# Strassen's method for half of the last output stage of a sparse-attention and FFN kernel, and one cast moved to another engine

## The chip, the cores and the metric

The kernel runs on one core of one Trainium2 chip. The metric is the device time of one execution in microseconds (us). Engines are named as in the profile: PE is the matrix engine TensorE, PEld its weight loads, DVE is VectorE, ACT is ScalarE, POOL is GpSimd, SP is SyncE, which here issues DMA. SBUF and PSUM are the two on-chip memories of the kernel's tiles; its matmuls write to the PSUM tiles, which the profile's lines name `ps_...`. A "bank" here is a PSUM tile, or the half of one, of 512 fp32 columns of 128 partitions.

## The reference, cut to what matters

```python
def _attn_ref(q, k, v):                       # (8, 8, 576, 64): batch, heads, tokens, head size
    ...                                       # causal; half of the heads local, half strided
    return np.matmul(attn, v)

def _moe_ref(x, w1, w2, w3, w_out):           # x: 4608 tokens x 512
    a = x @ w1                                # first FFN stage, 512 -> 1024
    b = x @ w2
    h = a * b @ w3
    return (h @ w_out).astype(np.float32)     # output, 1024 -> 512
```

Both kernels first fuse `w3 @ w_out` into one 1024x512 weight, called `w34`. What is left for a tile of 512 tokens is the first stage (`a`, `b` and their product `abt`) and the output stage `abt @ w34`. There are nine tiles, 0 to 8. The last two are finished after all attention work and form the tail of the execution.

## The kernel before: the parts that matter

The kernel records its operations in a planner, with the other operations that each depends on. The planner puts them into one fixed order per engine, from estimates of their durations. The framework then derives the semaphore waits between engines from the tiles that each instruction reads and writes, as the built programs of after and e3 show further down. This division is what the explanation turns on: **the planner knows the waits that the author entered, the built program has those that the framework derives.**

The first stage of the last two tiles (`tA`, `tB`) is done by Strassen's method for seven of its eight column blocks of 128. This method multiplies two 2x2 arrangements of blocks with seven block products in place of eight, and pays for it with sums and differences of blocks. Each block takes seven products, P1 to P7, which accumulate in three PSUM banks: A is one tile of its own, E and G are the two halves of one tile of two banks.

```python
SF = cfg.get("sf", ())                                  # (1, 2, 3, 4, 5, 6, 7): column blocks by Strassen
# ... sums and differences of x and of w1, w2 are made by DVE and POOL
def bk(x, kA=kA, kB=kB):
    return bank(*kA) if x == "A" else bank(*kB)[:, "EG".index(x)]
# ... in P5, the first time for a slot:
    seen[plan.slot[kB]] = bank(*kB, [P, 2, NT], FP32)   # one PSUM tile, E is [:, 0], G is [:, 1]
# ...
q1 = prod("P1", take=[kA], rank=R, extra=list(zs.values()))               # A = P1
q5 = prod("P5", take=[kB], rank=R + .1, extra=[q1])                       # G = P5
ce_ = vec("e", "ACT", ... copy("ACT", bk("E"), bk("A")), [q1, q5])        # E = P1
q6 = prod("P6", extra=[ce_], rank=R + .5)                                 # A += P6
c5 = vec("p5", "ACT", ... copy("ACT", new("p5"), bk("G")), [q5], ...)     # p5 to SBUF
q2 = prod("P2", extra=[q5 if n_ < 2 else ce_], rank=R + .6)               # E += P2
cu = vec("u2", "ACT", ... copy("ACT", new("u2"), bk("A")), [q6], ...)     # u2 to SBUF
q7 = prod("P7", extra=[cu], rank=R + 1)                                   # A += P7
g = vec("u4", "DVE", ... tensor_add(bk("G"), bk("G"), tmp["u2"]), [cu, c5], ...)
c11 = vec("c11", "ACT", ... copy("ACT", new("c11"), bk("E")), [q2], ...)  # E to SBUF
c22 = vec("c22", "DVE", ... tensor_add(new("c22"), bk("A"), tmp["p5"]), [q7, c5], ...)
q3 = prod("P3", extra=[g], rank=R + 1.1)                                  # G += P3
q4 = prod("P4", extra=[c22], rank=R + 1.2)                                # A += P4
# h1 = G * c11 and h2 = A * c22 go to abt of tA and tB
```

The lists at the ends are what the planner is told. The output stage is ordinary: for each block `ts` of 128 tokens, eight matmuls of 512 columns, a copy to SBUF and a store of 256 KB.

```python
for ts in range(NT // P):
    ...
    def fo(...):
        for ci in range(4 * hf, 4 * hf + 4):
            pin(nc.tensor.matmul(ps, big[("abt", t)][:, ci, bass.ds(ts * P, P)],
                                 w34[:, ci, bass.ds(n0, nw)], start=(ci == 0), stop=(ci == KF - 1)))
```

The softmax here doesn't subtract the row's maximum and nothing guards it: scores larger than these inputs give would overflow.

## Time and profile before

| | kernel before |
|---|---|
| time, three runs | 270.85 us median (270.61 to 271.14) |
| time of a fourth run, the profiled one | 270.36 us |
| span of its profile, granted clock | 268.3 us, 1.0 |
| tile 7's first product starts | 199.97 us |
| the tail (first product after tile 6's output) starts | 224.71 us |
| last matmul ends | 264.43 us |

The page's own lines are shown in the prediction, further down, with how they are read. Two things are worth seeing beside them. The first is a hole, a time in which TensorE starts nothing, in the timeline of TensorE (columns: start, duration, engine, line, operation, output and inputs, shapes, count):

```profile
236.65 0.59 PE L1053 MATMUL ps_Bw<-st,st 128*128 128x512 f16 x2
237.08 0.59 PE L1053 MATMUL ps_Aw<-st,st 128*128 128x512 f16 x2
237.79 0.59 PE L1053 MATMUL ps_Bw<-st,w2h 128*128 128x512 f16 x2
```

Matmuls overlap here (each of the first two lines lasts 0.59 us, and the second starts 0.43 us after the first), so their durations cannot be added; starts can be subtracted. From 236.65 to 237.08 are 0.43 us, two slots of 0.216 without a hole. From 237.08 to 237.79 are 0.71 us, so 0.28 us are lost. The third line carries no idle note, because by its modelled duration the line ahead of it ended just before. Every hole in this document is found in this way: the difference of two starts, less the count times 0.2157 us (512 columns), 0.1092 (256) or 0.056 (128). In the profiles of before and after matmuls that follow without a hole start 215 or 216 ns apart with 512 columns, 108 to 110 with 256 and 55 or 56 with 128; none starts less than 215 ns after one of 512 columns. The second thing is the end of GpSimd's work, in its timeline:

```profile
232.16 2.13 POOL L965 TENSOR_TENSOR st<-w1h,st 128x1024 f16<-128x1024 f16 x1
```

After 234.3 us this engine is idle, and the change uses that time.

### The profile page before, as it was taken

To read this page: it belongs to the slowest core of one execution; us is meant where nothing else is said; L and a number is where in the kernel's file an instruction comes from. 1 tells how busy PE (TensorE), PEld (TensorE's weight loads), DVE (VectorE), ACT (ScalarE), POOL (GpSimd) and SP (SyncE) were. 2 spreads that over 40 slices of the span, in tenths; PEclk is the share of its full clock that TensorE was granted. 3 is DMA by queue.
4 is the path that set the end of the run, shared out by engine and by line. 5 is a ranking of instruction groups with operands and counts; after the bars stand their busy time and mean duration, and the time that the engine had idled before them with its cause. 6 is when DMAs were issued, how large, how long until landed. Compare 5 with 4: busy or idle time off the path is not lost.

```text
span 268.3 us, 6079 instructions
## 1 busy us (share of the span) xinstructions
PE 256.9 (96%) x2251; PEld 140.3 (52%) x2251; DVE 179.0 (67%) x342; ACT 162.2 (60%) x293; POOL 168.9 (63%) x186
## 2 busy tenths in 40 slices
PE   7878799999999999999999999999999999999994
PEld 2457687545655555554554454455445554434443
DVE  6744565885787748866875788569748865678601
ACT  2780467774766785577477557764775576577241
POOL 6676897779979716955796369716989753900000
PEclk9999999999999999999999999999999999999999
DMA  6999899999799988899999998999996004000053
GB/s 247 322 365 288 294 353 353 326 266 290 255 287 211 175 205 243 188 167 283 228 184 180 264 248 182 189 252 235 162 189 198 2 0 156 0 2 0 0 197 121
DMA packets 72766, 54.41 MB, mean 203 GB/s; under 512 B 44256, under 2 KB 62048, under 8 KB 72736
## 3 DMA queue, kind: packets, MB, share of 16 engines
q1 hardware_dynamic: 72736, 54.02, 83.1%
q8 instruction: 18, 0.29, 0.5%
q14 instruction: 12, 0.10, 0.1%
HBM read 38.93 MB, written 9.44 MB: 180 GB/s over the span
## 4 chain that ended last, share of the span: by engine, by line
PE 86%; DMA 7%; POOL 2%; issue 1%; DVE 1%; ACT 1%; SPq 1%; POOLq 0%; DVEq 0%
PE ps_o L1155 23%; PE ps_b L1135 19%; PE ps_a L1119 18%; DMA st<-in_moe_w_dram 5%; PE ps_Aw L1053 4%; PE ps_S L795 4%; PE ps_Bw L1053 3%; PE ps_mm L670 3%; PE ps_X L843 3%; PE ps_X L831 3%; DMA st<-in_k_dram 2%; PE ps_U L924 2%; PE ps_T L748 2%; POOL w3n L314 1%; SPq L317 1%
## 5 line engine op out<-in xcount | busy, mean ns | idle before, releaser
L1155 PE MATMUL ps_o<-w,abt 128*128 128x512 f16 (+2 forms) x304 | 67.9, 368 | 0.0
L1135 PE MATMUL ps_b<-xT,w2h 128*128 128x512 f16 x232 | 59.4, 379 | 0.2 <-DVE kTL L312 0.2
L1119 PE MATMUL ps_a<-xT,w1h 128*128 128x512 f16 x232 | 59.6, 379 | 0.0
L310 ACT COPY asb<-ps_a 128x512 f32<-128x512 f32 x58 | 33.9, 587 | 30.1 <-PE ps_a L1119 29.0
L1141 DVE TENSOR_TENSOR abt<-ps_b,asb 128x512 f16<-128x512 f32 x58 | 39.9, 688 | 7.8 <-PE ps_b L1135 6.4
L314 POOL CAST xs<-st 80x1024 f16<-80x1024 f32 (+1 forms) x36 | 33.3, 940 | 18.3 <-DMA st<-in_k_dram 10.5
L812 ACT ACTIVATE ps_S<-ps_S 128x576 f32<-128x576 f32 (+2 forms) x56 | 32.8, 627 | 16.4 <-PE ps_S L795 16.4
L1155 PEld LDWEIGHTS <-abt 128*128 128x128 f16 x304 | 27.5, 98 | 28.2 <-issue 0.2
L904 DVE TENSOR_TENSOR xT<-ps_X,rcp 64x288 f16<-64x288 f32 x56 | 25.2, 450 | 18.3 <-ACT rcp L888 17.8
L1135 PEld LDWEIGHTS <-w2h 128*128 128x128 f16 x232 | 21.6, 98 | 23.7 <-issue 0.7
L310 ACT COPY osb<-ps_o 128x512 f32<-128x512 f32 (+1 forms) x36 | 20.2, 580 | 18.7 <-PE ps_o L1155 17.7
L314 POOL CAST v16L<-st 32x768 f16<-32x768 f32 (+1 forms) x32 | 26.3, 821 | 7.3 <-DMA st<-in_v_dram 5.7
L1119 PEld LDWEIGHTS <-w1h 128*128 128x128 f16 x232 | 20.2, 99 | 18.5
L819 DVE TENSOR_TENSOR ptm<-ps_S,maskL 128x576 f16<-128x576 f32 x28 | 19.9, 753 | 9.1 <-ACT ps_S L812 9.0
L867 DVE TENSOR_TENSOR xqs<-ps_X,rcq 96x384 f16<-96x384 f32 (+1 forms) x36 | 20.5, 568 | 1.2
L314 POOL CAST v16S<-st 72x1024 f16<-72x1024 f32 (+1 forms) x16 | 16.5, 1035 | 6.8 <-DMA st<-in_v_dram 6.8
L877 ACT ACTIVATE ps_X<-ps_X 64x576 f32<-64x576 f32 x28 | 17.6, 630 | 3.8 <-PE ps_X L831 3.2
L888 ACT ACTIVATE rcp<-ps_X 64x576 f32<-64x576 f32 x28 | 18.1, 647 | 0.9
L843 PEld LDWEIGHTS <-ptm 128*96 128x96 f16 (+1 forms) x224 | 14.6, 123 | 5.8 <-issue 0.2
L670 PE MATMUL ps_mm<-woh,xT 128*128 128x256 f16 x128 | 16.0, 273 | 1.3 <-POOL woh L314 1.3
L314 POOL CAST x<-st 128x1024 f16<-128x1024 f32 x14 | 14.4, 1036 | 4.4 <-DMA st<-in_k_dram 2.6
L819 DVE TENSOR_TENSOR ptm<-ps_S,maskK 72x576 f16<-72x576 f32 x20 | 14.1, 746 | 2.6 <-ACT ps_S L812 2.6
(113 smaller groups left out, 359.1 us busy)
## 6 DMA issues: line engine op xcount, KB each, us to landing
out_dram<-osb SPq DMA_DIRECT2D x35, 256.0 KB
st<-in_moe_w_dram SPq DMA_DIRECT2D x16, 512.0 KB
st<-in_v_dram SPq DMA_DIRECT2D x16, 288.0 KB
st<-in_v_dram SPq DMA_DIRECT2D x16, 256.0 KB
st<-in_q_dram SPq DMA_DIRECT2D x7, 512.0 KB
st<-in_k_dram SPq DMA_DIRECT2D x7, 512.0 KB
st<-in_q_dram SPq DMA_DIRECT2D x10, 256.0 KB
st<-in_k_dram SPq DMA_DIRECT2D x10, 256.0 KB
```

What stands on the lines that cost most here:

```text
L310: pin(nc.scalar.copy(out=out, in_=in_))
L314: pin(nc.gpsimd.tensor_copy(out=out, in_=in_))
L670: pin(nc.tensor.matmul(ps, w3T(kc)[:, js], big["woh"][:, kc, ns], start=(kc == 0), stop=(kc == KF - 1)))
L812: pin(nc.scalar.activation(out=sps, in_=sps, func=AF.Exp, bias=0.0, scale=scale))
L819: pin(nc.vector.tensor_mul(ptm[0:kr, 0:576].rearrange("p (h a x) -> p h a x", h=2, x=w), pte[0:kr].rearrange("p h (a x) -> p h a x", x=w), ...
L843: pin(nc.tensor.matmul(xps[0:w, h, i * 65:(i + 1) * 65], ptms[pslot][0:kr, c0:c0 + w], vt[0:kr, 2 * (hp % 2) + h, g * m + i, 0:D + 1], sta ...
L867: pin(nc.vector.tensor_mul(xqs[0:w, 0:m].rearrange("p i h d -> p h i d"), xv[:, :, :, 0:D], _ap(rcp, 0, [[rcp.ap[0][0], w], [4, 2], [1, m] ...
L904: pin(nc.vector.tensor_mul(o, i0, i1))
L1119: pin(nc.tensor.matmul(ps, w1h[:, ci, js], xT[ci][:, tok], start=(ci == 0), stop=(ci == KM - 1)))
L1135: pin(nc.tensor.matmul(ps, w2h[:, ci, js], xT[ci][:, tok], start=(ci == 0), stop=(ci == KM - 1)))
L1141: pin(nc.vector.tensor_mul(big[("abt", t)][:, jc, :], bank("f", f"b{t}_{jc}"), live[("asb", t, jc)]))
L1155: pin(nc.tensor.matmul(ps, big[("abt", t)][:, ci, bass.ds(ts * P, P)], w34[:, ci, bass.ds(n0, nw)], start=(ci == 0), stop=(ci == KF - 1)))
```

## The change

Its intent is to have TensorE do less in the tail. An output block of `tA` and one of `tB` are taken as a 2x2 problem and done by Strassen's method too: 28 matmuls of 256 columns for 16 of 512. This is done for two of the four blocks of each tile (`so=(0, 1)`). In the first stage another column block, 7 in place of 0, is left to the ordinary way. A cast of batch 7's `k` goes from GpSimd to ScalarE. The diff, cut to its core:

```diff
-  sf=(1, 2, 3, 4, 5, 6, 7), ...
+  sf=(0, 1, 2, 3, 4, 5, 6), ... so=(0, 1), ro=42,
+  ce={'ks7_3': 'ACT'})
 ...
-                     u2=2, p5=2, c11=2, c22=2))
+                     u2=2, p5=2, c11=2, c22=2, ob=4))
 ...
+    def out_strassen():
+        HN = DM // 2
+        ...  # T1..T4: differences of quarters of w34, {"POOL": 2150} each
+        for n_, ts in enumerate(SO):
+            ...  # Z1..Z4: sums of quarters of abt, Z3 on POOL, the others on DVE
+            def bk(x, kA=kA, kB=kB):
+                return (bank(*kA) if x == "A" else bank(*kB)[:, "EG".index(x)])[:, 0:HN]
+            ...
+            q1 = prod("P1", take=[kA], extra=sfirst)
+            q5 = prod("P5", take=[kB], extra=[q1], rank=.1)
+            ce_ = vec("e", AC, ... copy(e, bk("E"), bk("A")), [q1, q5])
+            q6 = prod("P6", extra=[ce_], rank=.5)
+            c5 = vec("p5", AC, ... copy(e, new("p5"), bk("G")), [q5], take=["p5"])
+            q2 = prod("P2", extra=[ce_], rank=.6)
+            cu = vec("u2", AC, ... copy(e, new("u2"), bk("A")), [q6], take=["u2"])
+            q7 = prod("P7", extra=[cu], rank=1)
+            g = vec("u4", DV, ... tensor_add(bk("G"), bk("G"), tmp["u2"]), [cu, c5], ...)
+            c22 = vec("c22", DV, ... tensor_add(new("o8")[:, HN:DM], bk("A"), tmp["p5"]), [q7, c5], ...)
+            c11 = vec("c11", AD, ... copy(e, new("o7")[:, 0:HN], bk("E")), [q2], take=["o7"])
+            q3 = prod("P3", extra=[g], rank=1.1)
+            q4 = prod("P4", extra=[c22], rank=1.2)
+            ...  # copies of G and A to the output rows, one store of each row block
 ...
+        if SO and t == tB:
+            out_strassen()
         for ts in range(NT // P):
+            if t in zs and ts in SO:
+                continue
```

More of the change, by code (lines that the diff above doesn't have):

```diff
@@ L41 @@
            pord=lambda b: (2, 3, 0, 1) if b < 2 else (0, 1, 2, 3), tsplit=False, dmaf=1.08, nhr=8, cast=dict(w1=dict(POOL=1040)),
-           first=('DVE', 'ACT', 'POOL'), early=0, pm=4, nx=4, nstg=8, new=(2, 3), lb=3, ll=4, nat={'POOL': 1160}, sf=(1, 2, 3, 4, 5, 6, 7), te={'POOL': 2150}, nr=(1, 25, 2, 0), te1='POOL', se=((3, 0), (3, 1), (1, 0), (2, 0), (4, 0)))
+           first=('DVE', 'ACT', 'POOL'), early=0, pm=4, nx=4, nstg=8, new=(2, 3), lb=3, ll=4, nat={'POOL': 1160}, sf=(0, 1, 2, 3, 4, 5, 6), te={'POOL': 2150}, nr=(1, 25, 2, 0), te1='POOL', se=((3, 0), (3, 1), (1, 0), (2, 0), (4, 0)), so=(0, 1), ro=42,
+           ce={'ks7_3': 'ACT'})
 def _ap(t: bass.AP, off_add, dims):
@@ L580, in fn @@
                 copy(e, t.rearrange("p c h d -> p h c d"), stg[key][0:nr])
-                x16[(b, nm, hp)] = t
+                x16[(b, nm, "s", hp)] = t
             c = cast("c" + key, key, ds, {"POOL": 825} if local else POOL, fn)
@@ L594, in ft @@
                 pin(nc.sync.dma_start(o.rearrange("x (c w) -> x c w", w=nr),
-                                      x16[(b, nm, hp)].rearrange("p c h d -> p (c h d)"), transpose=True))
+                                      x16[(b, nm, "s", hp)].rearrange("p c h d -> p (c h d)"), transpose=True))
             o = DTop[(b, nm, hp)] = plan.op(f"D{nm}{b}_{hp}", {"SP": 1300}, ft, deps=[c], dma=cfg.get("dtc", (1080, 1200))[0 if local else 1], store=True,
@@ L947 @@
     tk1, tk2 = bass.ds(tA * NT, NT), bass.ds(tB * NT, NT)
-    smul, sfirst = {}, []
+    smul, sfirst, mul = {}, [], {}
     if SF:
@@ L1003 @@
                 T[(i, 1)].deps.append(gate)
+        T1last = T[(4, 1)]
         SL = lambda j: (lambda c: St[j // 3][:, (j - 1) % 2 if j < 3 else j - 3, c])
@@ L1092, with ftt, ah, sv @@
         smul[(tA, jc)], smul[(tB, jc)] = h1, h2
+    SO = cfg.get("so", ()) if SF else ()
+    def out_strassen():
+        HN = DM // 2
+        hh = {(1, 1): (tA, 0), (1, 2): (tA, 4), (2, 1): (tB, 0), (2, 2): (tB, 4)}
+        W = {(i, j): w34[:, 4 * i - 4:4 * i, bass.ds(HN * (j - 1), HN)] for i in (1, 2) for j in (1, 2)}
+        T, Tt = {}, {}
+        for i, x, y in ((1, (1, 2), (1, 1)), (3, (2, 2), (1, 2)), (2, (2, 2), 1), (4, (2, 1), 2)):
+            def ftt(e, i=i, x=x, y=y):
+                if i in (1, 2):
+                    raw = stgs[plan.slot[("stg", f"O{i}")]].bitcast(FP16).rearrange("p (i k n) -> p i k n", i=2, k=4)
+                    Tt[i], Tt[{1: 3, 2: 4}[i]] = raw[:, 0], raw[:, 1]
+                b0 = Tt[y] if isinstance(y, int) else W[y]
+                eng = nc.gpsimd if e == "POOL" else nc.vector
+                pin(eng.tensor_sub(Tt[i], W[x], b0))
+            T[i] = plan.op(f"O{i}", {"POOL": 2150}, ftt, deps=w34op + [T1last, T.get(1), T.get(2)],
+                           take=[("stg", f"O{i}")] if i in (1, 2) else [], rank=14, lock=True)
+        def ah(i, j, ts):
+            t, c0 = hh[(i, j)]
+            return big[("abt", t)][:, c0:c0 + 4, bass.ds(ts * P, P)]
+        def sv(i, ts):
+            return xT[i - 1][:, 0:4 * NT].rearrange("p (k n) -> p k n", k=4)[:, :, bass.ds(ts * P, P)]
+        md = lambda t, k: [mul[(t, jc)] for jc in range(4 * k - 4, 4 * k)]
+        for n_, ts in enumerate(SO):
+            Sx = {}
+            for i in (3, 1, 2, 4):
+                def fss(e, i=i, ts=ts):
+                    eng = nc.gpsimd if e == "POOL" else nc.vector
+                    f = eng.tensor_add if i == 1 else eng.tensor_sub
+                    a0 = {3: lambda: ah(1, 1, ts), 1: lambda: ah(2, 1, ts), 2: lambda: sv(1, ts), 4: lambda: ah(1, 2, ts)}
+                    a1 = {3: lambda: ah(2, 1, ts), 1: lambda: ah(2, 2, ts), 2: lambda: ah(1, 1, ts), 4: lambda: sv(2, ts)}
+                    pin(f(sv(i, ts), a0[i](), a1[i]()))
+                d = {3: md(tA, 1) + md(tB, 1), 1: md(tB, 1) + md(tB, 2), 2: md(tA, 1), 4: md(tA, 2)}[i]
+                Sx[i] = plan.op(f"Z{i}_{ts}", {"POOL": 1150} if i == 3 else {"DVE": 430}, fss,
+                                deps=d + ([Sx[i // 2]] if i in (2, 4) else []), rank=3.9 + .01 * n_, lock=True)
+            kA, kB = ("f", f"Ao{ts}"), ("B", f"Bo{ts}")
+            prods = dict(P1=(lambda ts=ts: ah(1, 1, ts), lambda: W[(1, 1)], "A", md(tA, 1) + w34op),
+                         P5=(lambda ts=ts: sv(1, ts), lambda: Tt[1], "G", [Sx[1], T[1]]),
+                         P6=(lambda ts=ts: sv(2, ts), lambda: Tt[2], "A", [Sx[2], T[2]]),
+                         P2=(lambda ts=ts: ah(1, 2, ts), lambda: W[(2, 1)], "E", md(tA, 2)),
+                         P7=(lambda ts=ts: sv(3, ts), lambda: Tt[3], "A", [Sx[3], T[3]]),
+                         P4=(lambda ts=ts: ah(2, 2, ts), lambda: Tt[4], "A", md(tB, 2) + [T[4]]),
+                         P3=(lambda ts=ts: sv(4, ts), lambda: W[(2, 2)], "G", [Sx[4]]))
+            tmp = {}
+            def bk(x, kA=kA, kB=kB):
+                return (bank(*kA) if x == "A" else bank(*kB)[:, "EG".index(x)])[:, 0:HN]
+            def new(nm, tmp=tmp, ts=ts):
+                if nm[0] == "o":
+                    tmp[nm] = xT[plan.slot[("ob", f"{nm}o{ts}")]][:, 4 * NT:6 * NT].bitcast(FP32)
+                else:
+                    tmp[nm] = qkp.tile([P, HN], FP32, tag=TAG[nm], bufs=2, name=nm)
+                return tmp[nm]
+            def prod(nm, extra=(), take=(), rank=0, ts=ts, kA=kA, kB=kB, prods=prods, bk=bk):
+                lf, rt, x, d = prods[nm]
+                def fn(e):
+                    if nm == "P1":
+                        bank(*kA, [P, NT], FP32)
+                    if nm == "P5":
+                        live[kB] = seen[plan.slot[kB]]
+                    st_ = nm in ("P1", "P5")
+                    for c in range(4):
+                        pin(nc.tensor.matmul(bk(x), lf()[:, c], rt()[:, c], start=st_ and c == 0, stop=c == 3,
+                                             skip_group_check=not st_))
+                return plan.op(f"{nm}o{ts}", {"PE": 440}, fn, deps=d + list(extra), take=take,
+                               rank=100 + 24 * tA + cfg.get('ro', 30) + 3 * n_ + rank, soft=True)
+            def vec(nm, eng, fn, deps, give=(), take=()):
+                return plan.op(f"{nm}o{ts}", eng, fn, deps=deps, give=list(give),
+                               take=[("ob" if x[0] == "o" else x, f"{x}o{ts}") for x in take], rank=3 + .1 * n_)
+            AC, DV, AD = {"ACT": 370}, {"DVE": 400}, {"ACT": 370, "DVE": 380}
+            tk = {x: ("ob" if x[0] == "o" else x, f"{x}o{ts}") for x in ("u2", "p5", "o7", "o8")}
+            q1 = prod("P1", take=[kA], extra=sfirst)
+            q5 = prod("P5", take=[kB], extra=[q1], rank=.1)
+            ce_ = vec("e", AC, lambda e, bk=bk: copy(e, bk("E"), bk("A")), [q1, q5])
+            q6 = prod("P6", extra=[ce_], rank=.5)
+            c5 = vec("p5", AC, lambda e, bk=bk, new=new: copy(e, new("p5"), bk("G")), [q5], take=["p5"])
+            q2 = prod("P2", extra=[ce_], rank=.6)
+            cu = vec("u2", AC, lambda e, bk=bk, new=new: copy(e, new("u2"), bk("A")), [q6], take=["u2"])
+            q7 = prod("P7", extra=[cu], rank=1)
+            g = vec("u4", DV, lambda e, bk=bk, tmp=tmp: pin(nc.vector.tensor_add(bk("G"), bk("G"), tmp["u2"])),
+                    [cu, c5], give=[tk["u2"]])
+            c22 = vec("c22", DV, lambda e, bk=bk, new=new, tmp=tmp: pin(
+                nc.vector.tensor_add(new("o8")[:, HN:DM], bk("A"), tmp["p5"])), [q7, c5], take=["o8"], give=[tk["p5"]])
+            c11 = vec("c11", AD, lambda e, bk=bk, new=new: copy(e, new("o7")[:, 0:HN], bk("E")), [q2], take=["o7"])
+            q3 = prod("P3", extra=[g], rank=1.1)
+            q4 = prod("P4", extra=[c22], rank=1.2)
+            c12 = vec("c12", AD, lambda e, bk=bk, tmp=tmp: copy(e, tmp["o7"][:, HN:DM], bk("G")), [q3, c11], give=[kB])
+            c21 = vec("c21", AD, lambda e, bk=bk, tmp=tmp: copy(e, tmp["o8"][:, 0:HN], bk("A")), [q4, c22], give=[kA])
+            for t, o, c in ((tA, "o7", c12), (tB, "o8", c21)):
+                plan.op(f"st{o}_{ts}", {"SP": 450}, lambda e, o=o, t=t, ts=ts, tmp=tmp: pin(
+                    nc.sync.dma_start(out_r[t * (NT // P) + ts], tmp[o])), deps=[c], give=[tk[o]], rank=4.5, dma=750,
+                        store=True)
@@ L1144 @@
                                 give=[("f", f"b{t}_{jc}"), ("asb", f"{t}_{jc}")], rank=4))
+        if t in zs:
+            mul.update({(t, jc): m for jc, m in enumerate(muls)})
+        if SO and t == tB:
+            out_strassen()
         for ts in range(NT // P):
+            if t in zs and ts in SO:
+                continue
             last = t == NTILE - 1 and ts == NT // P - 1
```

## The prediction

> **What bounds the kernel now.** I read the page first, for the engine shares and the chain, then the chain of waits in order of time, then the timeline of TensorE from 224 us on, and last the groups kept apart by form. The page says that TensorE carries the time:
>
> ```profile
> span 268.3 us, 6079 instructions
> PE 256.9 (96%) x2251; PEld 140.3 (52%) x2251; DVE 179.0 (67%) x342; ACT 162.2 (60%) x293; POOL 168.9 (63%) x186
> POOL 6676897779979716955796369716989753900000
> PE 86%; DMA 7%; POOL 2%; issue 1%; DVE 1%; ACT 1%; SPq 1%; POOLq 0%; DVEq 0%
> ```
>
> The reader is to see that TensorE (PE) is busy 96% of the span and 86% of the chain, and that GpSimd (POOL) does nothing in the last five of 40 slices (6.7 us each), which is where the change gives it work. Busy time of PE is an overlap of pipelined matmuls, so I take the cost of a matmul from the chain, where each piece is a difference of starts:
>
> ```profile
> 32.59 1.75 PE ps_mm L670 x16
> 145.82 3.46 PE ps_o L1155 x16
> 234.55 0.58 ACT ps_Bw L310
> 235.18 0.59 PE ps_Aw L1053 x2
> 236.42 0.59 ACT c L310
> 237.04 0.71 DVE ps_Bw L1076
> 237.79 0.59 PE ps_Bw L1053 x2
> 253.17 10.83 PE ps_o L1155 x60
> 264.08 0.68 DVE osb L312 x2
> ```
>
> From these: 3.46/16 = **0.216 us** per slot of 512 columns, 1.75/16 = **0.109 us** per slot of 256 columns with its own weight load. The three pieces on ACT and DVE between 234.5 and 237.8 are the few places at the end where TensorE waits: inside the Strassen products of the first FFN stage. After 253.17 the output matmuls run without a hole; then one small copy and the last store, about 3.5 us, end the span.
>
> How many holes are there? From the timeline, the tail starts at 224.71, and the last 512-wide product before the closing run of output matmuls is issued at 253.00 (252.57 plus two slots). In between stand 12 ordinary, 98 Strassen, 4 ordinary and 12 output matmuls, 126 in all: 126 x 0.216 = 27.2 us against 28.3 us. So **about 1.1 us of holes** lie in the tail. The largest is this:
>
> ```profile
> 234.35 0.59 PE L1053 MATMUL ps_Aw<-xT,w1h 128*128 128x512 f16 x2
> 235.18 0.59 PE L1053 MATMUL ps_Aw<-st,st 128*128 128x512 f16 x2 [0.23 <-ACT ps_Bw L310]
> ```
>
> The second line starts 0.83 us after the first, whose two slots are worth 0.43: 0.40 us lost, to a copy on ACT that has to empty the bank.
>
> [...] the 128x512 f16 sums of two SBUF tiles take 0.42 us, those that read PSUM 0.68 to 0.70. [...]
>
> **The change, part by part.** I compared the order of instructions in the two built programs. On TensorE it is identical for the first 3715 of some 4500 rows, that is up to batch 7's attention near 200 us. Everything before that stays; the change is read from the last 70 us.
>
> (a) *Removed and added matmuls.* An output block of 128 tokens is 8 matmuls of 512 columns. A pair of such blocks (one of each of the last two tiles) is 16 x 0.216 = 3.46 us. By Strassen it is 7 products of 4 matmuls of 256 columns, 28 x 0.109 = 3.05 us. Saved 0.40 us a pair, and two of the four pairs are done so: **-0.8 us** on TensorE, all on the path. [...]
>
> (b) *Added work beside it.* GpSimd: four differences of 128x1024 of the fused output weight, like the existing ones of 2.12 us, so 8.5 us, plus two sums of 128x512 at 1.15. Its present last work begins at 225.6 and takes 8.6 us; by my steps it begins at 227.5 in the new order, so the weights are ready at about 244.6 and the two sums at 247. The first product that needs them stands at 254: **hidden**, by 7 us or more. The cast moved to ACT frees 1.04 us of GpSimd near 197.6, before a queue that later waits for DVE anyway (idle 4.62 at 217.6, 4.42 at 225.6): worth nothing by itself. DVE: six sums of 0.42 us, then four additions and four copies of 256 columns from PSUM, some 0.42 each (so long take the 128x256 copies of before); ACT: eight copies of 256 columns at some 0.37 (the 128x256 casts of before). Together 6 us on DVE and 3 on ACT, less the four 512-column copies of 0.58 that go. After 250 us DVE is busy 3.9 and ACT 4.7 of 18.3 us in the kernel before (busy time by stretch), so there is room.
>
> (c) *The first new wait.* Strassen's first mixed product needs the last elementwise product of the FFN and then one DVE sum: last Strassen matmul issued at X, DVE sees it 0.2 us later, 0.68 for the product, 0.05 + 0.42 for the sum, 0.05 to TensorE: X + 1.4 us. The order puts two ordinary output groups, 8 x 0.216 = 1.73 us, in between. **Covered, with 0.3 us to spare.** Stepping the 15 further groups in the order of the program with 0.37 (ACT), 0.42 (DVE), 0.2 to leave TensorE and 0.05 to get back, each bank copy is done 0.2 to 0.6 us before the product that overwrites the bank, since the two blocks are interleaved and two ordinary output groups are used as fillers. No hole that I can find.
>
> (d) *The reordered first stage.* Leaving column block 7 instead of 0 to the ordinary way moves two ordinary groups of tile 7 from ahead of the Strassen products to among them. Ahead of them now stand only three products that need no sum (1.30 us instead of 2.59), while batch 7's last attention block also comes later, by two output groups (1.73 us), because the cast sits on ACT in front of the exponentials. I step that chain with the durations of the trace: last attention product issued at 222.98, exp and log on ACT until 224.92, normalisation 0.91, sum 0.42: ready at 226.4, wanted at 226.01. A matmul that doesn't need it comes first there, so 0.2 us of hole. Stepping on through 50 groups I find one more, 0.4 us, where the third column block's bank copy is waited for; the 0.40 and 0.28 us holes of before at 235 and 237 are filled by the interleaved ordinary groups. **Holes 0.6 us instead of 1.1: -0.5 us.** This is the softest term.
>
> (e) *The end.* The last block (three narrow parts) is the same and so is the last store. But 256 KB stores now end closer together: the last two blocks' stores are issued some 1.5 us before the narrow ones, where before only one was. The profile moves 300 GB/s at its best in the tail, so 512 KB take 1.7 us: 0 to 0.3 us late, I take **+0.1**.
>
> Sum: -0.8 - 0.5 + 0.1 = **-1.2 us**, span 267.1. The timed runs lie above the span, 270.85 against 268.3, and that difference stays: **269.65 us**.
>
> **Rivals.** *The wait takes the saving's place.* Each new block has a serial chain of some 7 bank copies and sums; if leaving and re-entering TensorE costs 0.1 us more than I step, three or four of the 15 groups stop, 0.2 us each, and (d) may save nothing: 270.2 to 270.5. For it: the first stage of the kernel before, same algorithm, lost 1.1 us so. Against it: half-size copies, and fillers. *The attention chain becomes the bound* near 224: if the cast on ACT delays batch 7's exponentials by its full 1.05 us and the schedule has no slack there, another 0.5 to 1 us hole opens before the first mixed product: 270.5 to 271. Against it: ACT was idle 0.85 us at exactly that spot (199.1 to 199.95), so only 0.2 us is passed on. *GpSimd is late*: if the new weight differences slow DVE[...], or end after 254. Against it: DVE's 0.68 to 0.70 us operations were as long before 234, with GpSimd at work, as after; and 7 us of slack. [...] *A slightly larger gain*: all holes vanish, -1.9 us: 269.0.
>
> **Range and chances.** 269.65, with 269.0 (no holes at all) and 270.4 (holes as many as before, and late stores) as ends. 2% would be 5.4 us; the whole tail holds only 1.1 us of holes and the saving on TensorE is 0.8, so faster by 2% can't come out of these numbers, and slower by 2% needs a wait five times as long as any in the tail: 0.01 and 0.01.
>
> **What would show it.** The matmuls of the new products: 24 more, slots of 0.109 us. The difference of starts over the whole closing stage: about 0.8 us less for the same sums. GpSimd's last instruction near 247, well before the first product that reads its weights. PE lines with an idle note in the new products would show the first rival, one at the first product from the summed tiles the second. The last matmul should be issued about 1.2 us earlier and the time from it to the end stay at 3.5 to 3.8 us. Wrong would be: an output store that holds a buffer, a lower granted clock, or different order before 200 us.

Passages that no trace or run of this case shows are cut from the prediction, and the cuts are marked: most of a paragraph on slots and on DVE, a remark on the cost of extra matmuls, and the way in which GpSimd's work might slow DVE, with what that would cost. No term of the sum is among them: -0.8 (a), -0.5 (d) and +0.1 (e) make the -1.2 us, and so 269.65.

The figures for hardware that the steps use are in the profile of before. DVE's 128x512 sums of two SBUF tiles take 0.42 us (three, at 224.24 to 225.58), its 128x512 operations on PSUM 0.68 to 0.70. To leave TensorE took 0.20 us at 234.55: ACT's copy starts so long after the products it waits for are out (233.92 and two slots, 234.35). To get back took 0.05: the product at 235.18 starts so long after that copy's end. From one DVE sum to the next that reads it, at 224.70, were 0.04. And between 256 and 258 us DMA moved 301 GB/s, the 300 of (e).

## The result

The kernel after took 269.73 us in the median of four runs (269.42 to 270.01); the kernel before took 270.73 in four runs beside them (270.36 to 271.14). The ratio is 0.9963, with a 95% interval from 0.9943 to 0.9982. A ratio here is the mean time of one kernel's fast runs over the mean of the other's of the same rounds, so it isn't quite the ratio of the medians that are quoted. Both profiles were taken at full clock (1.0 and 0.998). All outputs are right.

Here are the lines of the page of the kernel after that answer to those of before:

```profile
span 267.8 us, 6151 instructions
PE 256.5 (96%) x2275; PEld 143.0 (53%) x2275; DVE 184.3 (69%) x356; ACT 163.1 (61%) x298; POOL 178.7 (67%) x191
POOL 6676997679979827974796379627979542997000
PE 13%; DVE 1%; ACT 1%; issue 0%; DVEq 0%
```

TensorE has 24 more matmuls, as it should. GpSimd works two slices longer. The last line is not a result: the chain could only be followed back over 15% of the span and breaks off there, so this line can't be set against the 86% of before.

So a time of 269.73 against 269.65 predicted. **It would be easy to stop here. But the 0.5 us between the two spans do not lie where the prediction had put them.** I cut both executions at marks that both have: the start of tile 7's first product, the start of the tail, the end of the last matmul, and the end of the span.

| stretch, us | before | after |
|---|---|---|
| start of the span to tile 7's first product | 199.97 | 199.49 |
| from there to the tail | 24.74 | 24.75 |
| the tail on TensorE | 39.72 | 39.79 |
| of it in slots (tail less holes) | 38.60 | 37.84 |
| of it in holes | 1.12 | 1.95 |
| last matmul to the end | 3.87 | 3.77 |
| tile 7's first product to the end | 68.33 | 68.31 |

The page gives the span to 0.1 us, so the last two rows are good to 0.05; computed from the packed traces, the last row is 68.35 and 68.29.

The first row holds nearly the whole difference of the spans, and there the two programs give TensorE the same instructions in the same order. It comes with the loads at the start. A cast of FFN weights on GpSimd shows it, first before, then after (the number in brackets is the idle time ahead of it, and what ended that):

```profile
27.39 1.04 POOL L314 CAST w3n<-st 128x1024 f16<-128x1024 f32 x1 [1.48 <-DMA st<-in_moe_w_dram]
```

```profile
26.90 1.04 POOL L315 CAST w3n<-st 128x1024 f16<-128x1024 f32 x1 [1.39 <-DMA st<-in_moe_w_dram]
```

The same cast, after a wait for the same load, starts 0.49 us earlier in after, and tile 7's first product 0.48 us earlier. Ten of the eleven experiments further down agree with this: set against before's, the start of this cast and that of tile 7's first product are shifted by the same amount, to 0.02 us (in e5 something is added between 34 and 37 us). From 37 us on to tile 7 the shift of TensorE no longer changes. An earlier load, that of `q`, does not predict it: e8 has the earliest cast of `q`, at 7.11 us where before's is at 7.78, and yet its tile 7 starts 0.46 us later.

The times differ by more than the spans. Time less span is 2.06 us in the profiled run of before and 1.76 in that of after. This goes with the kernel: it is 2.00 to 2.19 us in 43 executions without the Strassen products of the output stage (before, e1, e4, e5), and 1.66 to 1.82 in 35 with them. So some 0.35 us of the 1.0 that was timed lie outside what the profile shows. They repeat, but no run here says what they are.

In the part of the program that the change touches, 0.76 us of slots were saved and 0.83 us of holes were added. Where are those? In the first stage three are left, 0.21, 0.39 and 0.28 us; the middle one is this, in TensorE's timeline of after:

```profile
232.68 0.59 PE L1055 MATMUL ps_Aw<-xT,w1h 128*128 128x512 f16 x2
233.50 0.59 PE L1055 MATMUL ps_Aw<-st,st 128*128 128x512 f16 x2 [0.23 <-ACT ps_Bw L311]
```

That sums to 0.88, so the first stage has become a little better than before's 1.12. The other two are new, in the Strassen products of the output stage (L1168):

```profile
256.24 0.60 PE L1168 MATMUL ps_Bw<-st,xT 128*128 128x256 f16 x4
256.68 0.60 PE L1168 MATMUL ps_Ao<-st,xT 128*128 128x256 f16 x4
257.41 0.60 PE L1168 MATMUL ps_Bw<-w,xT 128*128 128x256 f16 x4
...
258.71 0.60 PE L1168 MATMUL ps_Bw<-w,abt 128*128 128x256 f16 x4
259.15 0.60 PE L1168 MATMUL ps_Ao<-st,xT 128*128 128x256 f16 x4
260.37 0.60 PE L1168 MATMUL ps_Bw<-w,xT 128*128 128x256 f16 x4 [0.61 <-DVE xT L313]
```

Four slots of 256 columns are 0.44 us. P3 of the first block (the third line) starts 0.73 us after P7 (the second): 0.29 lost. P3 of the second block (the last line) starts 1.22 us after its P7: 0.78 lost. Together 1.07 us. By the code, P3 accumulates in bank G and needs u4, an addition in that bank. Its note names something else: "DVE xT L313" is a copy of bank E to the output rows. DVE's timeline shows the two, and ACT's the copy of u2 that u4 needs:

```profile
259.42 0.43 DVE L1188 TENSOR_TENSOR ps_Bw<-ps_Bw,u 128x256 f32<-128x256 f32 x1 [0.89 <-PE ps_Bw L1168]
259.89 0.42 DVE L313 COPY xT<-ps_Bw 128x256 f32<-128x256 f32 x1
```

```profile
258.48 0.37 ACT L311 COPY u<-ps_Ao 128x256 f32<-128x256 f32 x1 [0.44 <-PE ps_Ao L1168]
```

The operand u2 was there at 258.85. The addition u4 started only at 259.42, 0.57 us later, and what ended its wait is "PE ps_Bw", which is P2, started at 258.71: a product that writes to E, the other bank. Then P3, which writes to G, waited for a copy that reads E. None of these waits is needed by the data.

### The profile page after: what moved, and what is told of

It is laid out like the page before. It is cut to its first block, busy times and chain, and to the rows that moved or that the text cites. A ratio compares the mean times of both kernels' runs of the same rounds, so it can differ in the third digit from the quotient of the medians.

```text
span 267.8 us, 6151 instructions
## 1 busy us (share of the span) xinstructions
PE 256.5 (96%) x2275; PEld 143.0 (53%) x2275; DVE 184.3 (69%) x356; ACT 163.1 (61%) x298; POOL 178.7 (67%) x191
## 5 line engine op out<-in xcount | busy, mean ns | idle before, releaser
L1269 PE MATMUL ps_o<-w,abt 128*128 128x512 f16 (+2 forms) x272 | 61.3, 367 | 0.0
L315 POOL CAST xs<-st 80x1024 f16<-80x1024 f32 (+1 forms) x35 | 32.3, 939 | 18.0 <-DMA st<-in_k_dram 11.4
L1269 PEld LDWEIGHTS <-abt 128*128 128x128 f16 x272 | 24.4, 98 | 23.7
L311 ACT COPY osb<-ps_o 128x512 f32<-128x512 f32 (+1 forms) x32 | 18.1, 581 | 15.2 <-PE ps_o L1269 15.1
```

What stands on the lines that cost most here:

```text
L311: pin(nc.scalar.copy(out=out, in_=in_))
L315: pin(nc.gpsimd.tensor_copy(out=out, in_=in_))
```

## The experiments

**The theory (tied banks).** E and G are halves of one PSUM tile, and in the built program users of one bank wait for the earlier user of the other. Besides the waits that the data need, the built program has this chain, each step of it from E to G or back: P5 before the copy A to E, this before the copy of p5, this before P2, this before u4, this before the copy of c11, this before P3. Of these the planner's lists have the first alone (`[q1, q5]`). I read u4's wait in the built program: it is for the count that P2 reaches. A rebuild of after's kernel shows all six as semaphore waits. In the rebuild of e3, described below, u4 waits for the copy of u2 alone, and P3 no longer for the copy of E. The theory says that two tiles of one bank each remove both new holes, and most of those in the first stage, in both kernels.

**Rivals.** (1) The chain is the true one of the data, and leaving and re-entering TensorE simply takes longer than I stepped. (2) The order is at fault: the planner has put P3 too close to what it needs, whatever the reason. (3) GpSimd or the cast moved to ACT holds up DVE or ACT. And beside them: the gain of 1.0 us that was timed first is real, though the two profiles don't show it.

### First set: repeats, and the banks untied in both kernels

`e1_before_again` is the kernel before, unchanged, and `e2_after_again` is the kernel after, unchanged.

> The kernel before, unchanged, timed against itself: how much of the 0.4% is scatter. Both theories: ratio 1.000 within 0.2%. In the two profiles at hand the stretch from tile 7's first product to the end is 68.3 us in both kernels, and the 0.5 us between the spans lie in the first 20 us, in the landing of loads; if so, start-up here scatters by some 0.5 us too, and the stretch stays at 68.3.

> The changed kernel again. If the change saves about 1 us, as the first timed runs and my prediction have it, ratio 0.996 to 0.997. If the profile pair is right that it saves nothing from tile 7 on, ratio 0.999 to 1.000, and the stretch from tile 7's first product to the end is 68.3 us again with 1.9 us of holes in TensorE.

`e3_after_split` is the kernel after with this edit, and `e4_before_split` the kernel before with the same:

```diff
+    psb = [tc.tile_pool(name="psb", bufs=1, space=bass.MemoryType.PSUM, reuse_waits="tile")]
+    psb.append(psb[0].__enter__())
 ...
         def bk(x, kA=kA, kB=kB):
-            return bank(*kA) if x == "A" else bank(*kB)[:, "EG".index(x)]
+            return bank(*kA) if x == "A" else live[kB]["EG".index(x)]
 ...   # in P5
-                        seen[plan.slot[kB]] = bank(*kB, [P, 2, NT], FP32)
+                        if not seen:      # the two-bank tiles of the attention end here, E and G tiles begin
+                            psb[0].__exit__(None, None, None)
+                            psb[:] = [tc.tile_pool(name="pse", bufs=1, space=..., reuse_waits="tile")]
+                            psb.append(psb[0].__enter__())
+                        live[kB] = seen[plan.slot[kB]] = [
+                            psb[1].tile([P, NT], FP32, tag=f"{x}{plan.slot[kB]}", name=f"ps_{x}w") for x in "EG"]
```

The cut leaves out two lines: the output stage's `bk` gets the same edit, and the attention's two-bank tiles move to the new pool `psb`; from tile 7's first product to the tail both kernels still take 24.75 us. What the planner is told is the same, and a comparison of the built programs shows the same order of instructions on every engine. Only waits differ.

> The changed kernel, same instructions in the same order, but the two PSUM banks of a Strassen group are two tiles instead of the halves of one tile, so that waits between one bank's user and the other's fall away. Theory A (the holes come from these needless waits): the holes of 0.39, 0.28, 0.29 and 0.78 us at 233, 239, 257 and 260 us go, 0.2 to 0.4 us stay; 1.4 to 1.7 us faster than the changed kernel. Rival B (the copies and sums themselves take too long): the holes stay, same time within 0.2 us.

> The kernel before with the same split and nothing else. Theory A: its holes of 0.15, 0.40, 0.18 and 0.28 us go, 0.9 to 1.1 us faster than before; the split pair then differs by the saving on TensorE alone, 0.8 us. Rival B: same time as before.

All four ran on one chip, in five rounds. The kernel before took 271.26 us there (270.25 to 271.87, 11 runs).

| run | median us (range, 6 runs) | ratio, 95% interval | tail on TensorE | holes in it | tile 7's first product to the end |
|---|---|---|---|---|---|
| e1_before_again | 270.6 (269.49 to 272.38) | 0.9987 (0.9957 to 1.0017) | 39.73 | 1.11 | 68.38 |
| e2_after_again | 270.62 (270.22 to 272.86) | 0.9994 (0.9964 to 1.0024) | 39.79 | 1.95 | 68.32 |
| e3_after_split | 268.67 (267.34 to 269.27) | 0.9904 (0.9878 to 0.9931) | 38.05 | 0.21 | 66.54 |
| e4_before_split | 269.4 (268.32 to 269.94) | 0.9935 (0.9911 to 0.9958) | 38.63 | 0 | 67.28 |

What follows. First, the repeat doesn't show the gain that was timed first: 0.9994, and an unchanged kernel against itself gives 0.9987. The interval, 0.9964 to 1.0024, still allows the 0.35 us outside the span (0.13%). The stretches are far steadier than the times: 68.33 and 68.38 us for before, 68.31 and 68.32 for after. What scatters is the start: tile 7's first product starts at 199.97 and 199.02 in the two profiles of before, at 199.49 and 200.38 in those of after.

Second, the theory holds. Here are P7 and P3 of both blocks again, in the timeline of TensorE with the banks untied; the tile names now tell E from G:

```profile
257.27 0.60 PE L1174 MATMUL ps_Ao<-st,xT 128*128 128x256 f16 x4
257.71 0.60 PE L1174 MATMUL ps_Gw<-w,xT 128*128 128x256 f16 x4
...
259.46 0.60 PE L1174 MATMUL ps_Ao<-st,xT 128*128 128x256 f16 x4
259.89 0.60 PE L1174 MATMUL ps_Gw<-w,xT 128*128 128x256 f16 x4
```

Both are 0.44 us apart: no hole. And u4 of the first block, in DVE's timeline, with the copy of E on ACT:

```profile
257.00 0.43 DVE L1194 TENSOR_TENSOR ps_Gw<-ps_Gw,u 128x256 f32<-128x256 f32 x1 [1.48 <-ACT u L313]
```

```profile
257.04 0.37 ACT L313 COPY xT<-ps_Ew 128x256 f32<-128x256 f32 x1
```

The addition is now released by the copy of u2, as the data ask, and the copy of E runs beside it (257.04 to 257.41 against 257.00 to 257.43), where it had to wait for it before; P7 writes to A meanwhile, from 257.27 on, and the results are correct. The durations are the same as in the kernel after, 0.43 and 0.37, so the steps had not become quicker: rival 1 is out, and rival 2 in its plain form, too, since the order is the same. Of 1.95 us of holes 0.21 are left, and 1.74 us were the tied banks. In the kernel before it is all of the 1.1 us: the kernel before had the same fault, in its first stage, and I had read those holes as the cost of the method.

Third, the matmul saving is real once the holes are gone: 38.63 less 38.05 is 0.58 on TensorE, with 0.21 us of the latter in the hole at the first mixed product, so 0.79 by slots, and 67.28 less 66.54 is 0.74 to the end. The prediction had 0.8. By time the two are further apart by the 0.35 us outside the span; their medians, 269.4 and 268.67, hold the scatter of the start besides.

### Second set: one part at a time

The last was timed in three rounds, on a chip where the kernel before took 270.02 us (269.79 to 271.37, 7 runs).

`e5_no_out` leaves out the Strassen output stage and keeps the reordered first stage and the cast:

```diff
-  so=(0, 1), ro=42,
+  so=(), ro=42,
```

> The changed kernel without the Strassen of the output stage: only the cast on ACT, and column block 7 in place of 0 as the ordinary one. The first stage's order should be that of the changed kernel, so its three holes of 0.21, 0.39 and 0.28 us stay and the two of 0.29 and 0.78 go with the output products: 0.88 us against 1.12 before. From the start of the tail (after tile 6's last output matmul) to the last matmul: 39.5 us, against 39.72 before and 39.79 in the changed kernel. If that holds, the output stage alone costs 0.3 us net, in spite of 0.8 us less matmul.

Measured: 270.6 us once. The tail on TensorE took 39.53 us, with holes of 0.21, 0.39 and 0.27, all in the first stage; 68.36 to the end. The output stage has none. So the first stage in its new order saves 0.25 us of holes (1.12 to 0.87), the 1.07 us come with the new output stage, and that stage's matmul saving of 0.8 is used up by them: with it or without it, 68.31 or 68.36 us.

`e6_no_cast` gives the cast back to GpSimd:

```diff
-  ce={'ks7_3': 'ACT'})
+  ce={})
```

> The changed kernel with the late cast back on GpSimd. In the built program the attention of batch 7 and the ordinary groups then stand as in the kernel before, so the first stage should have that kernel's holes, 1.1 us, the output stage the changed kernel's 1.07: 2.2 us of holes, 40.0 us from the start of the tail to the last matmul, 0.2 us more than with the cast on ACT. If GpSimd were the bound, it would be more: its last work would end late and the first mixed output product would wait.

Measured: 269.77 us once. The tail took 40.15 us, with 2.33 us of holes, and 68.66 to the end. In the first stage they are 0.15, 0.40, 0.18, 0.27 and 0.06, just those of the kernel before. Column blocks 7 and 0 are exchanged here too, so what (d) saves doesn't come with the exchange alone but needs the cast on ACT; the cast without the exchange was not run. With the cast on ACT batch 7's last attention products start at 222.25, with it on GpSimd at 220.47, and the ordinary groups stand in another order among the products. The cast on ACT is worth some 0.35 us here (two holes more, 0.16 and 0.06, stand between the stages). The two in the output stage are there as ever, 0.28 and 0.77, so neither GpSimd nor the cast causes them: rival 3 is out.

`e7_planned_waits` keeps the tied banks and tells the planner of four of the five waits that it doesn't know, in the output stage alone (the fifth, from the copy of A to E to the copy of p5, joins two copies that ACT makes in this order anyway):

```diff
-  q2 = prod("P2", extra=[ce_], rank=.6)
+  q2 = prod("P2", extra=[ce_, c5], rank=.6)
-  g = vec("u4", DV, ..., [cu, c5], ...)
+  g = vec("u4", DV, ..., [cu, c5, q2], ...)
-  c11 = vec("c11", AD, ..., [q2], ...)
-  q3 = prod("P3", extra=[g], rank=1.1)
+  c11 = vec("c11", AD, ..., [q2, g], ...)
+  q3 = prod("P3", extra=[g, c11], rank=1.1)
```

> The changed kernel with one tile per pair of banks as it is, but the needless waits of the output stage entered in the list of dependences from which the order is made. Theory A: the order now fills the 0.29 and 0.78 us holes with other matmuls and they shrink to 0.3 us or less in sum; the first stage keeps its 0.88. 39.0 us from the start of the tail to the last matmul. Rival B: the holes move elsewhere in the output stage, 39.8 us.

Measured: 270.15 us once. The output stage has no hole; those of the first stage are as in after, 0.21, 0.39 and 0.28. The planner now puts an ordinary group ahead of P3:

```profile
257.68 0.60 PE L1168 MATMUL ps_Ao<-st,xT 128*128 128x256 f16 x4
258.12 1.03 PE L1269 MATMUL ps_o<-w,abt 128*128 128x512 f16 x4
258.98 0.60 PE L1168 MATMUL ps_Bw<-w,xT 128*128 128x256 f16 x4
```

The tail falls to 38.73 us, but the time from the last matmul to the end rises from 3.77 to 4.43. The likely reason, not tested, is that the Strassen blocks now finish among the last copies and stores: DVE's last copy of a Strassen block starts 0.8 us before the last matmul's end (263.14 of 263.97), where in after it was 1.7 us (262.30 of 264.03). To the end it is 67.91, 0.4 less than after and 1.4 more than with untied banks. So order can hide needless waits, at a price; the size of the 1.07 us is confirmed from a second side, as all of it went when only the planner's knowledge changed.

`e8_split_3of4` is e3 with a third block by Strassen: `so=(0, 1, 2)`.

> The changed kernel with split tiles and three of four token blocks by Strassen. TensorE saves another 0.4 us: 37.65 us from the start of the tail to the last matmul if no hole opens. But its last product then ends the order, and the last copy and store are of 256 KB and not of 64: the end grows from 3.75 to 4.3 us or more. So within 0.3 us of the split with two blocks, either way.

Measured: 268.91 us (268.42 to 269.15, 4 runs), ratio 0.9946 (0.991 to 0.9981). The tail took 37.82 us with 0.34 us of holes, 66.47 to the end, against 66.54 with two blocks. The 0.4 us that a third pair saves in slots is met by 0.13 us more of holes and 0.15 us more at the end (3.89 against 3.74). The two stayed within 0.3 us, as expected, but the growth of the end to 4.3 us or more did not come.

### Third set: is there a better version?

`e9_split_no_cast` is e3 with the cast on GpSimd (`ce={}`).

> Split tiles, two of four blocks by Strassen, and the late cast back on GpSimd. The attention of batch 7 and the ordinary groups ahead of the Strassen products then stand as in the kernel before, so that the last hole of the split kernel, 0.21 us at the first mixed product, should go: 37.85 us from the start of the tail to the last matmul, 0.2 us less than the split kernel with the cast on ACT. If GpSimd is short of time without that microsecond, a wait on it appears instead.

The next kernel is that of e8, with the cast on ACT:

> The split kernel with three of four blocks again (cast on ACT), beside the one without the cast: 37.8 us from the start of the tail to the last matmul, 66.5 from tile 7's first product to the end, as in its first run; a repeat to see whether that stretch repeats to 0.1 us on another chip where the time does not.

So it is a repeat of e8 on another chip, and it came out as expected: 37.79 and 66.51 us, against 37.82 and 66.47 in e8. `e11_split_3of4_gp` is the kernel with the cast on GpSimd.

> Split tiles, three of four blocks, cast on GpSimd: both gains. 37.6 us from the start of the tail to the last matmul, 66.3 us from tile 7's first product to the end, against 68.3 in both kernels of the study: 0.992 to 0.993 of the kernel before.

| run | median us (range) | ratio, 95% interval | tail on TensorE | holes | tile 7's first product to the end |
|---|---|---|---|---|---|
| e9_split_no_cast | 268.32 (267.52 to 269.33, 6 runs) | 0.9914 (0.9888 to 0.9939) | 37.90 | 0.08 | 66.43 |
| e10 (e8 again) | 267.42 (one run) | | 37.79 | 0.28 | 66.51 |
| e11_split_3of4_gp | 269.08 (268.29 to 270.7, 6 runs) | 0.9946 (0.9918 to 0.9974) | 37.73 | 0.23 | 66.38 |

The kernel before took 270.74 us there (269.62 to 271.27, 11 runs). e9 came out as expected: 37.90 us for 37.85, the hole at the first mixed product gone, and no wait on GpSimd. e11's stretch was near its expectation (37.73 for 37.6, 66.38 for 66.3), its ratio of 0.9946 was above the expected 0.992 to 0.993. The four versions with untied banks lie between 66.38 and 66.54 us to the end and can't be told apart; all are some 1.8 us below both kernels, by time 0.5 to 1.0%. None reaches 2%. The cast on ACT, worth 0.35 us with tied banks, costs 0.15 on TensorE with them untied (38.05 against 37.90). e9 is the simplest of them, and the interval of its ratio lies wholly below those of both kernels' repeats.

## Why the prediction was right or wrong

By time it was right, by its reason only in part, and the close agreement is luck. 269.73 us were measured and 269.65 predicted, within 269.0 to 270.4, and "within 2%" had 0.98. But the repeat of after took 270.62, just above the range, and the part of the program that the change touches became less than 0.1 us shorter, not 1.2. Between the two profiled runs, 270.36 and 269.56, the 0.8 us are 0.48 of start, 0.30 outside the span and 0.02 of that part. The prediction had neither of the first two. Its base helped as well: it set the median of three runs, 270.85, against the span of a fourth, so the 2.55 us between them are 2.06 within one run, and "that difference stays" failed, as it fell to 1.76.

- **What bounds the kernel** was right: TensorE, with 1.1 us of holes in the tail. The "cost" of those holes was right, their cause was not asked for. I had seen that TensorE waits "to a copy on ACT that has to empty the bank" and not that this copy waited without need.
- **(a) The matmuls, −0.8 us: right.** The slots of the tail went from 38.60 to 37.84, and 0.74 us to the end between the two untied kernels.
- **(b) The added work is hidden: right.** GpSimd's differences and sums ended at 246.24, where I had put about 247, and the first product that reads them started at 253.63, without a hole:

```profile
243.97 2.27 POOL L1133 TENSOR_TENSOR xT<-abt 128x512 f16<-128x512 f16 x2
...
253.63 0.60 PE L1168 MATMUL ps_Bw<-st,xT 128*128 128x256 f16 x4
```

- **(c) The failed step: "No hole that I can find."** The first new wait was covered, as stepped. The further groups lost 1.07 us, at P3 of both blocks. The durations in the step were right (0.37 on ACT and 0.42 or 0.43 on DVE); the waits were wrong. I took them from the data and from the lists that the planner is given, and the built program has more. A sign that the prediction itself had named for its first rival showed it: the new product at 260.37 carries an idle note of 0.61 us. e3 removes these waits and the holes go; e7 tells the planner of them and the holes go too.
- **(d) The first stage, −0.5 us: the direction right, the size about half.** Holes of 0.6 us were predicted and 0.88 measured. The two that I had found are there with their sizes, 0.2 at the first mixed product and 0.4 at a bank copy. The third, 0.28 us, I had missed. With untied banks the 0.39 and the 0.28 are gone and the 0.21 stays, so the latter is the attention's and the others are the tied banks'. e6 shows besides that the exchange of column blocks brought nothing without the cast. Calling this "the softest term" was fair, but (c) was softer, and the range had no room for it.
- **(e) The end, +0.1 us: off, without weight.** It was 3.77 us against 3.87, −0.1.

With measured terms the sum is −0.76 (a), +1.07 (c), −0.24 (d) and −0.1 (e), which is −0.03 us; 68.33 to 68.31 was measured. The first rival, "the wait takes the saving's place", is what happened, even in its place (the new blocks' copies and sums), though in two groups rather than in three or four of 0.2 us, and not because re-entering TensorE took longer: P3 starts 0.05 us, as stepped, after the copy of E that it waits for, in both blocks (257.36 to 257.41 and 260.31 to 260.37). I had argued against it with half-size copies and fillers; neither helps against a wait on the wrong bank. The attention chain cost the 0.21 us hole that (d) had counted and no more, and GpSimd was no bound. One slip had no weight: 5.4 us are not five times any wait in the tail but five times all its holes together, over 13 times the longest (0.40).

What stays open: why the loads at the start scatter by over a microsecond between executions (in the thirteen profiles tile 7's first product started between 199.02 and 200.76 us, and all of it arises in the first 37 us), and what the 0.35 us outside the span are. The first is the same for every version and I did not study it; the second comes with the new output stage.

## What to carry to other kernels

Where accumulators in different PSUM banks are used by different engines at different times, make each a tile of its own: in this framework the waits follow tiles, and here two banks in one tile cost 1.1 us in one kernel and 1.74 in the other. When stepping a new chain by hand, take its waits from the built program, not from the data, and when a trace shows a wait, ask whether its releaser touches the same bank. And when a change concerns the last quarter of an execution whose start scatters, compare that stretch between common marks: it repeated here within 0.1 us, while medians of the same kernel differed by up to 1.2 (the kernel before: 270.02 to 271.26). Look also at time less span, run by run, as it needn't be the same for two kernels.
